# Score groups of two chunks in one visit of the dense layer, in a fused retention and gated layer kernel

## The chip, the cores and the metric

The kernel runs on one core of a Trainium2 chip. The metric is the device time of one launch in microseconds; a kernel's time is the median of several runs. One execution of each kernel was also taken by the hardware profiler, and the profile's span is the part of that execution from the first to the last instruction of the program.

## The reference

A retention layer (attention with a decay and without a softmax) over 8 batches of 8 heads, 576 positions and 64 features, then a dense layer with the activation h cos(h) over its 4608 tokens of 512 features:

```python
scores = scale * np.matmul(q, k.transpose(0, 1, 3, 2))
gamma = 1.0 - 2.0 ** (-5.0 - np.arange(H))
Dmat = np.where(rel >= 0, gamma[:, None, None] ** rel[None], 0.0)   # rel = i - j
attn = np.matmul(scores * Dmat[None], v)          # 8 x 8 x 576 x 64
x = attn.transpose(0, 2, 1, 3).reshape(4608, 512)
h = x @ w_in                                      # 512 -> 2048
out = (h * np.cos(h)) @ w_out                     # 2048 -> 512
```

## The kernel before

The positions of a batch are cut into five chunks, four of 128 and a last one of 64. The decay is split into a factor on v, a factor on the output and a causal mask, so that within a chunk the scores need only the mask, and everything before the chunk sits in a running state (k transposed times v, one 64 x 64 block a head).

For a chunk r of batch b there are two steps. `scores(b, r)` (line 405) is one group of eight TensorE matmuls, one a head, with 64 rows of contraction; the two heads of a pair sit on the two halves of the array and write two PSUM banks, sc0 and sc1. VectorE then multiplies each bank by the mask into a bf16 tile (line 428), `rt`, of which there are two pairs in turn. `rest(b, r)` (line 433) is the remainder: four matmuls of the state with q (tile names kqt, sb; not for chunk 0), eight of the masked scores with v (rt, vb), both into the bank po; eight that add the chunk to the state bank st (vb, kqb; not for chunk 4); two ScalarE copies of the state into SBUF (line 471) and one VectorE product that takes po into the token tile xt (line 476). `stage(b, r)` is `rest(b, r)` followed by `scores(b, r + 1)`.

The dense layer works in nine blocks of 512 tokens. `mlp1(j, dt)` (line 489), sixteen times a block, is four matmuls of w_in with xt into a bank, a ScalarE sine (line 504) and a VectorE product of the two into the tile gt (line 507). `mlp2(j, st, part)` (line 514) is four of the sixteen matmuls of one output tile of 128 tokens; four parts fill one bank, which ScalarE then copies out (line 538) for a store. Both take their banks from the four dense banks mm0 to mm3 in rotation:

```python
def bank(self):
    while self.n_mm % 4 in self.open.values():
        self.n_mm += 1
    self.n_mm += 1
    i = (self.n_mm - 1) % 4
    return self.MM[i], self.bMM[i]
```

`open` holds the bank of an output tile that is not complete; only such a bank is passed over. Before anything is written into a bank, its former readers must be done.

The order of each engine's instructions is the order in which the program emits them, and a helper adds the semaphore waits that the buffers call for. So the place of the retention work among the matmuls of the dense layer is written out by hand, in `emit`. In block j from 1 to 6 the batch b = j + 1 is worked on: the program runs mlp1 sixteen times, and then n = 0 to 15 output visits, `mlp2(j, n // 4, n % 4)`. Ahead of the visits n = 0, 3, 6, 9, 12 comes a part of batch b: at n = 0 the rest of the former batch's chunk 4 and the scores of chunk 0; at n = 3, 6, 9 and 12 the rest of chunk n/3 - 1 and the scores of chunk n/3. The document calls block j's part of the program stage j. Block 0 and the first two batches are ordered differently and are not touched.

Keys and queries of batches 2 to 7 reach their transposed form (tile kqt) by DMA: `prep` (line 320) casts a chunk on GpSimd and issues a transposing DMA on SyncE's queue (line 328). These run ahead of TensorE, in the order of batches and chunks, with every buffer doubled by the parity of the batch.

Of the kernel before, what the change touches and what calls it, by code (L numbers as in the profile page):

```python
# [16 lines left out]
NCH = (S_ + CH - 1) // CH  # L17
# [106 lines left out]
class _Kernel:  # L124
# [425 lines left out]
    def emit(self):  # L550
        s = self.s
        self.load("k", 0, 0)
        self.load_q0()
        for x, r in (("v", 0), ("k", 1), ("v", 1), ("k", 2), ("k", 3), ("v", 2), ("v", 3),
                     ("k", 4), ("v", 4)):
            self.load(x, 0, r)
        self.consts_a()
        for c in range(3):
            self.consts_b(c)
        for r in range(2):  # L560
            self.casts(0, r)
        self.cast("pool", "k", 0, 2)
        self.w_in_load(0)
        self.cast("pool", "k", 0, 3)
        self.w_in_load(1)
        for r in (2, 3):
            self.vmul("pool", 0, r)
            self.w_in_load(r)
        self.w_in_load(4)
        self.casts(0, 4)  # L570
        for i in range(NWO):
            w = self.w_out_load(i)
            if i == 0:
                for r in range(NCH):
                    for x in "kv":
                        self.load(x, 1, r, after=[w])
            if i == 1:
                self.load_qx(1)
        for r in range(NCH):
            self.casts(1, r)  # L580

        po, st = (self.PO, self.bPO), (self.ST, self.bST)
        self.spin(30, po)
        evict = self.turn_k_pe(0, 0, st, "dve")
        for c in range(NP):
            self.cast_q0(c)
        evict()
        for c in range(NP):
            self.turn_q(0, c, "act")
            self.spin((8, 5, 5, 16)[c], po)  # L590
        self.consts_b(3)
        self.scores(0, 0)
        self.spin(10, po)
        self.turn_k(0, 1)
        self.spin(8)
        self.rest(0, 0)
        self.scores(0, 1)
        self.spin(16)
        self.turn_k(0, 2)
        self.rest(0, 1)  # L600
        self.scores(0, 2)
        self.turn_k(0, 3)

        s.op("act", lambda e: e.activation(self.JUNK.ap(), self.C_PIH.ap(), AF.Sin), reads=[self.bC])  # L604
        self.spin(8)
        self.scores(0, 3, sc=[self.bank(), self.bank()])
        self.rest(0, 2)
        self.spin(4)
        self.rest(0, 3, self.bank())
        self.spin(8, po)  # L610

        for dt in range(16):
            self.mlp1(0, dt)
            if dt == 2:
                self.turn_k(0, 4)
            if dt == 4:
                self.scores(0, 4)
            if dt == 6:
                self.rest(0, 4)

        self.fetch(2)
        for r in range(NCH):
            self.feed(2, r, 3 if r == NCH - 1 else 1)
        spare = [(self.PO, self.bPO), (self.SC[0], self.bSC[0]), (self.SC[1], self.bSC[1]),
                 (self.ST, self.bST)]
        for n in range(16):
            self.mlp2(0, n % 4, n // 4)
            if n == 7:
                for c in range(NP):
                    self.turn_q(1, c, ("act", "dve")[c % 2], spare[c])  # L630
            if n in (8, 10):
                self.turn_k(1, n // 2 - 4, spare[0])
            if n in (9, 12):
                self.scores(1, n // 3 - 3)
            if n == 13:
                self.rest(1, 0)
            if n == 14:
                self.turn_k(1, 2, spare[0])
        self.flush()
        self.rest(1, 1)  # L640
        self.spin(10)

        n = 3 * 64 + CH
        for dt in range(16):
            self.mlp1(1, dt, 0, n)
            if dt in (1, 7, 13):
                self.scores(1, 2 + dt // 6, True)
            if dt in (3, 9):
                self.turn_k(1, 3 + dt // 6)
            if dt in (5, 11):  # L650
                self.rest(1, 2 + dt // 6)
        for dt in range(16):
            self.mlp1(1, dt, n, TB - n)
        for j in range(1, NTB):
            b = j + 1
            for dt in range(16 if j > 1 else 0):
                self.mlp1(j, dt)
                if b < B_ and dt % 3 == 2:
                    self.feed(b, dt // 3)
            for n in range(16):  # L660

                if n == 0 and b <= B_:
                    self.rest(b - 1, NCH - 1)
                if b < B_:
                    if n == 0:
                        self.scores(b, 0)
                    elif n % 3 == 0 and n < 15:
                        self.stage(b, n // 3 - 1)
                self.mlp2(j, n // 4, n % 4)
        self.flush()  # L670
        for name, (h, n) in s.dsem.items():
            if name[0] == "o":
                self.nc.scalar.wait_ge(h, n)
# [28 lines left out]
```

## Time and profile before

| | us |
|---|---|
| median of 3 runs (316.6 to 317.02) | 316.94 |
| the profiled execution | 316.4 |
| its span | 314.7 |
| TensorE matmuls busy | 303.5 |
| TensorE weight loads busy | 159.6 |
| VectorE busy | 174.1 |
| ScalarE busy | 162.3 |
| GpSimd busy | 93.1 |

How to read the lines that follow: PE is TensorE, PEld its weight loads, DVE VectorE, ACT ScalarE, POOL GpSimd and SP SyncE; L401 is line 401 of the kernel. `sc<-kqt` names the tile that is written and those that are read, with buffer numbers left out. All of TensorE's groups go through one helper, so lines 401 and 403 hold all matmuls but a group's last and the last, and the tiles tell them apart. Shapes such as 64*128 are the rows and columns of the array that the instruction uses. Matmuls are pipelined, so the shown durations of neighbours overlap; the distance between starts is the time that one takes from the next. A few matmul records are missing from the trace.

The stages in the span: the output visits of stage 1 begin at 73.9 us, of stage 2 at 106.5, of stage 3 at 139.1, of stage 4 at 171.7, of stage 5 at 204.4 and of stage 6 at 237.0. TensorE is busy 32.53 of the 33 us from 139 to 172.

### The profile page before, as it was taken

How to read it: one execution, taken by the hardware profiler on the slowest of the kernel's cores; microseconds unless marked ns; L12 is line 12 of the kernel's file. 1: busy time of each engine (PE TensorE's matmuls, PEld its weight loads, DVE VectorE, ACT ScalarE, POOL GpSimd, SP SyncE). 2: the span in 40 equal slices, each digit the busy share in tenths (PEclk: the TensorE clock that was granted, in tenths of full speed). 3: DMA queues.
4: the chain of work that ended last, by engine and by line, in shares of the span. 5: the costliest groups of instructions: out<-in, count | busy, mean ns of one | idle time of the engine just before them, and what ended most of it. 6: DMA issues, size and time to landing. Idle time of an engine off the chain costs nothing.

```text
span 314.7 us, 6424 instructions
## 1 busy us (share of the span) xinstructions
PE 303.5 (96%) x2516; PEld 159.6 (51%) x2552; DVE 174.1 (55%) x301; ACT 162.3 (52%) x290; POOL 93.1 (30%) x128
## 2 busy tenths in 40 slices
PE   6989999999999999999999999999999999999996
PEld 5754455666544455445544554455444544444442
DVE  3567624787527743685458644765387438405700
ACT  7566525785337533763277236723473257316711
POOL 2692027535454434453445424210000000000000
PEclk9999999999999999999999999999999999999999
DMA  7999999999999999999999999940001100120021
GB/s 218 213 168 204 203 220 247 264 192 209 212 256 183 217 210 247 217 224 217 259 208 202 225 204 221 172 85 35 33 0 38 66 33 0 42 94 1 12 83 74
DMA packets 142814, 48.85 MB, mean 155 GB/s; under 512 B 132544, under 2 KB 137664, under 8 KB 142784
## 3 DMA queue, kind: packets, MB, share of 16 engines
q1 hardware_dynamic: 132320, 34.22, 59.7%
q0 software_dynamic: 5280, 4.78, 9.5%
q10 hardware_dynamic: 5184, 9.44, 8.9%
q8 instruction: 20, 0.33, 0.4%
q14 instruction: 10, 0.08, 0.1%
HBM read 36.70 MB, written 9.44 MB: 147 GB/s over the span
## 4 chain that ended last, share of the span: by engine, by line
PE 90%; DMA 2%; DVE 2%; ACT 2%; issue 2%; SPq 1%; POOL 0%; DVEq 0%
PE mm L401 59%; PE mm L403 20%; PE po L401 6%; PE sc L401 4%; DMA kn<-in_k_dram 2%; PE st L401 1%; DVE gt L507 1%; DVE rt L428 1%; SPq L276 1%; ACT sb L471 0%; DVE xt L476 0%; ACT L604 0%; ACT osb L538 0%; ACT kqt L365 0%; SPq L267 0%
## 5 line engine op out<-in xcount | busy, mean ns | idle before, releaser
L507 DVE TENSOR_TENSOR gt<-mm,cb 128x512 bf16<-128x512 f32 (+2 forms) x160 | 101.1, 637 | 66.2 <-ACT cb L504 63.6
L401 PE MATMUL mm<-xt,win 128*128 128x512 bf16 (+2 forms) x468 | 116.0, 358 | 1.0 <-DVE xt L476 0.3
L504 ACT ACTIVATE cb<-mm,c_pih 128x512 bf16<-128x512 f32 (+2 forms) x160 | 101.9, 645 | 27.8 <-PE mm L403 27.0
L401 PE MATMUL mm<-wout,gt 128*128 128x512 bf16 x408 | 111.8, 380 | 2.3 <-issue 1.7
L401 PEld LDWEIGHTS mm<-xt,win 128*128 128x128 bf16 x480 | 44.6, 98 | 48.8 <-DVE gt L507 2.3
L401 PEld LDWEIGHTS mm<-wout,gt 128*128 128x128 bf16 x432 | 39.3, 98 | 45.1
L403 PE MATMUL mm<-xt,win 128*128 128x512 bf16 (+2 forms) x160 | 57.2, 358 | 0.3
L538 ACT ACTIVATE osb<-mm 128x512 f32<-128x512 f32 x36 | 21.5, 597 | 68.0 <-PE mm L403 68.0
L403 PE MATMUL mm<-wout,gt 128*128 128x512 bf16 x144 | 54.6, 379 | 0.5
L308 POOL TENSOR_TENSOR vb<-vn,wv 128x512 bf16<-128x512 f32 (+1 forms) x40 | 41.7, 1043 | 29.2 <-DMA vn<-in_v_dram 24.7
L428 DVE TENSOR_TENSOR rt<-sc,mk 128x512 bf16<-128x512 f32 (+1 forms) x78 | 45.8, 625 | 4.8 <-PE sc L403 4.8
L476 DVE TENSOR_TENSOR xt<-po,up 128x512 bf16<-128x512 f32 (+1 forms) x39 | 24.7, 634 | 41.9 <-PE po L403 41.8
L471 ACT ACTIVATE sb<-st 64x256 bf16<-64x256 f32 x64 | 24.2, 378 | 40.1 <-PE st L403 38.7
L318 POOL CAST kqb<-kn 128x512 bf16<-128x512 f32 (+1 forms) x40 | 24.4, 611 | 65.2 <-DMA kn<-in_k_dram 56.2
L318 POOL CAST kqb<-qn 128x512 bf16<-128x512 f32 (+1 forms) x30 | 18.5, 615 | 17.7 <-DMA qn<-in_q_dram 17.5
L403 PEld LDWEIGHTS mm<-xt,win 128*128 128x128 bf16 x160 | 15.7, 98 | 15.7
L403 PEld LDWEIGHTS mm<-wout,gt 128*128 128x128 bf16 x144 | 14.1, 98 | 17.0
L401 PE MATMUL po<-rt,vb 128*64 128x128 bf16 (+1 forms) x273 | 15.2, 220 | 0.0
L401 PE MATMUL sc<-kqt 64*128 64x128 bf16 (+1 forms) x273 | 14.7, 215 | 0.0
L401 PEld LDWEIGHTS po<-kqt,sb 128*128 128x128 bf16 x124 | 8.6, 98 | 7.8 <-DVE rt L428 1.6
L401 PEld LDWEIGHTS po<-rt,vb 128*64 128x64 bf16 (+1 forms) x273 | 9.3, 108 | 5.9 <-DVE rt L428 2.1
L401 PE MATMUL po<-kqt,sb 128*128 128x128 bf16 (+1 forms) x124 | 11.2, 213 | 0.4 <-DVE rt L428 0.2
(88 smaller groups left out, 133.2 us busy)
## 6 DMA issues: line engine op xcount, KB each, us to landing
out_dram<-osb ACTq DMA_DIRECT2D x36, 256.0 KB, 3.3
kn<-in_k_dram SPq DMA_DIRECT2D x32, 256.0 KB, 4.7
vn<-in_v_dram SPq DMA_DIRECT2D x32, 256.0 KB, 5.3
qn<-in_q_dram SPq DMA_DIRECT2D x24, 256.0 KB, 4.8
wout<-in_moe_w_out_dram POOLq DMA_DIRECT2D x4, 512.0 KB, 14.5
win<-in_moe_w_in_dram POOLq DMA_DIRECT2D x3, 512.0 KB, 8.2
qn<-in_q_dram SPq DMA_DIRECT2D x4, 288.0 KB, 4.7
kn<-in_k_dram SPq DMA_DIRECT2D x8, 128.0 KB, 3.5
```

The costliest lines, as they stand in the source:

```text
L276: s.dma("sp", f"q0_{c}", lambda e: e.dma_start(dst, src), writes=[self.bQN[c]])
L308: self.s.op(eng, lambda e: e.tensor_tensor(bass.AP(self.VB[i][r], 0, v3), self.staged("v", r, v3[1:]), bass.AP(self.WV, r * H_, [[NCH * H_ ...
L318: self.s.op(eng, lambda e: e.tensor_copy(o, f), reads=[self.bST32[x][r]], writes=[bt[i][r]])
L401: self.nc.tensor.matmul(o, a, b, **kw)
L403: return s.done("pe", self.nc.tensor.matmul(o, a, b, **kw), reads, writes)
L428: self.s.op("dve", lambda e: e.tensor_tensor(bass.AP(self.RT[k][hp], 0, p3), bass.AP(sc[0], 0, p3), bass.AP(self.MK, 0, [[CH, ck], [0, NP] ...
L471: s.op("act", lambda e: e.activation(bass.AP(self.SB[r % 2], 64 * hp * 512 + 64 * hp, [[512, 64], [128, NP], [1, D_]]), bass.AP(self.ST, 6 ...
L476: s.op("dve", lambda e: e.tensor_tensor(bass.AP(self.XT, t0, [[NP * XR, 128], [XR, NP], [1, ck]]), bass.AP(po, 0, [[512, 128], [CH, NP], [ ...
L504: s.op("act", lambda e: e.activation(co, mo, AF.Sin, bias=self.C_PIH.ap(), scale=1.0), reads=[bm, self.bC], writes=[bcb])
L507: s.op("dve", lambda e: e.tensor_tensor(bass.AP(g, dt * TB + o, [[16 * TB, 128], [1, n]]), mo, co, ALU.mult), reads=[bm, bcb], writes=[bg])
L538: s.op("act", lambda e: e.activation(o.ap(), m.ap(), AF.Copy), reads=[bm], writes=[bo])
```

## The change

From batch 2 on, the scores of two chunks are taken one behind the other: chunks 0 and 1 at n = 0, chunks 2 and 3 at n = 7, chunk 4 alone at n = 13. The second group of a pair takes its two banks from the four dense banks by `bank()`. The rests come at n = 4, 7, 10 and 13; the rest of chunk 4 stays at the next stage's n = 0.

```diff
                 if b < B_:
-                    if n == 0:
-                        self.scores(b, 0)
-                    elif n % 3 == 0 and n < 15:
-                        self.stage(b, n // 3 - 1)
+                    if n in (4, 7, 10, 13):
+                        self.rest(b, n // 3 - 1)
+                    if n in (0, 7):
+                        self.scores(b, n // 3)
+                        self.scores(b, n // 3 + 1, sc=[self.bank(), self.bank()])
+                    elif n == 13:
+                        self.scores(b, NCH - 1)
                 self.mlp2(j, n // 4, n % 4)
```

| n | before | changed |
|---|---|---|
| 0 | rest 4 of b - 1, scores 0 | rest 4 of b - 1, scores 0, scores 1 |
| 3 | rest 0, scores 1 | |
| 4 | | rest 0 |
| 6 | rest 1, scores 2 | |
| 7 | | rest 1, scores 2, scores 3 |
| 9 | rest 2, scores 3 | |
| 10 | | rest 2 |
| 12 | rest 3, scores 4 | |
| 13 | | rest 3, scores 4 |

In stages 1 to 6 the rotation then gives the second score group mm2 and mm3, output tiles 0 and 2 the bank mm0 and tiles 1 and 3 the bank mm1, where before the four output tiles had a bank each. No matmul, copy, product or DMA is added or dropped.

## The prediction

> **What bounds the kernel now.** I read the page first: busy shares, then the chain that ended last.
>
> ```profile
> span 314.7 us, 6424 instructions
> PE 303.5 (96%) x2516; PEld 159.6 (51%) x2552; DVE 174.1 (55%) x301; ACT 162.3 (52%) x290; POOL 93.1 (30%) x128
> ...
> PEclk9999999999999999999999999999999999999999
> ...
> PE 90%; DMA 2%; DVE 2%; ACT 2%; issue 2%; SPq 1%; POOL 0%; DVEq 0%
> PE mm L401 59%; PE mm L403 20%; PE po L401 6%; PE sc L401 4%; DMA kn<-in_k_dram 2%; PE st L401 1%; DVE gt L507 1%; DVE rt L428 1%; SPq L276 1%; ACT sb L471 0%; DVE xt L476 0%; ACT L604 0%; ACT osb L538 0%; ACT kqt L365 0%; SPq L267 0%
> ```
>
> TensorE makes 90% of the chain at the full granted clock; scores (sc) are 4% of it. Next, the waits of TensorE's two rows between 74 and 259 us, the stretch in which batches 2 to 7 run their chunk visits (stages 1 to 6):
>
> ```profile
> PE mm L401 <- issue: 1.6, 10, 0.2
> PE mm L401 <- DVE gt L507: 0.3, 2, 0.2
> ...
> PEld po L401 <- DVE rt L428: 2.1, 5, 0.4
> ```
>
> Twelve waits of the matmuls, none over 0.2 us: gaps of one missing matmul record each, with a little more, not stalls. The five before a weight load of po stand where n = 3 goes from the dense layer straight to rt matmuls; the masks had ended 0.25 us before. So there TensorE's time is the sum of its instructions and of what it loses between them, and a saving inside a visit reaches the end undiminished. That loss is in the timeline of TensorE, here the visits n = 0 and n = 3 of stage 4:
>
> ```profile
> 171.52 0.38 PE L403 MATMUL mm<-xt,win 128*128 128x512 bf16 x1
> 171.73 0.28 PE L401 MATMUL po<-kqt,sb 128*128 128x64 bf16 x4
> 171.94 0.31 PE L401 MATMUL po<-rt,vb 64*64 64x64 bf16 x7
> 172.06 0.19 PE L403 MATMUL po<-rt,vb 64*64 64x64 bf16 x1
> 172.19 0.39 PE L401 MATMUL sc<-kqt 64*128 64x128 bf16 x7
> 172.37 0.22 PE L403 MATMUL sc<-kqt 64*128 64x128 bf16 x1
> 172.52 0.82 PE L401 MATMUL mm<-wout,gt 128*128 128x512 bf16 x3
> ...
> 175.46 0.29 PE L401 MATMUL st<-vb,kqb 128*64 128x64 bf16 x7
> 175.55 0.20 PE L403 MATMUL st<-vb,kqb 128*64 128x64 bf16 x1
> 175.68 0.39 PE L401 MATMUL sc<-kqt 64*128 64x128 bf16 x7
> ```
>
> Columns: start, time, engine, line, names, array shape, count. Durations overlap, so I price by starts. A score group starts 172.19, its eighth matmul 172.37, the dense layer after it 172.52: a slot of 0.33. The eight run in pairs; the exact starts of the four pairs stand 0.066, 0.056 and 0.056 us apart. The step from the last pair to the dense layer is 0.148 instead of 0.056: leaving the 64*128 shape costs 0.09. From the last st to the scores it is 0.13 against 0.03 within st.
>
> **The change, part by part.** Per batch:
>
> 1. Visits n = 3 and n = 9 lose their score group (rest alone moves on to n = 4 and n = 10). Then st is followed by the dense layer instead of by scores. Does leaving st cost the same? The mixed layer of stage 1 has it:
>
> ```profile
> 59.97 0.20 PE L403 MATMUL st<-vb,kqb 128*64 128x64 bf16 x1
> 60.10 0.58 PE L401 MATMUL mm<-xt,win 128*128 128x320 bf16 x3
> ```
>
> 0.13 again. So each removes the whole slot: -0.330.
>
> 2. Visits n = 0 and n = 7 get a second group of eight behind the first in the same shape: four more pairs at 0.056 = +0.224. No row has two groups on end. From below, the eighth's start less the first's, 0.18, is all that a group could take if its first pair came free; from above 0.33, if the new group (other banks, a wait of its own) paid for leaving and entering like a separate one. I take 0.224: nothing changes shape between the groups, and po to st, two groups of one shape, step by 0.05 only.
>
> 3. n = 13 does what n = 12 did; the moved rests have the same dense neighbours. No matmul, copy, product or DMA is added or dropped.
>
> Sum: 2 x (0.224 - 0.330) = -0.21 per batch, six batches: **-1.27 us**. From the bounds: 12 x (0.18 - 0.33) = -1.8 and 12 x 0 = 0. The profiled execution took 316.4 (span 314.7 and 1.7 around it), so it would become 315.1; the median of the runs is 316.94, 0.54 above that execution, and becomes **315.67**.
>
> A page has a rule for the step: the Trainium skill, "TensorEngine Tiling (Array Packing)", section Key Properties, says that a change of tiling mode drains the engine, and "TensorE: Matmul & The Clock Gate", section Step-by-step, gives a drain about 128 cycles, which at 2.4 GHz is an estimate of 0.053 us. By that, twelve mode changes fewer bring 0.64 us; the row says 0.09 for one, and decides. Against the change speaks the second page's section "A second HAM failure mode": groups that cycle through PSUM banks, with small idle gaps between, let the clock be gated to half. The page's row of granted clock shows 9 in all 40 slices through sixty such visits, so I price it at nothing; one such window (3.4 us by the page) would cost 1.7 us and turn the sign.
>
> **New waits.** The second group uses two of the four dense banks. In stages 2 to 6 they are those of dt = 12 and 13, and the output matmuls of n = 0 now take the bank of dt = 14 instead of dt = 12; all of TensorE queues behind these. The gt product of dt = 14 ends at 172.55 in stage 4 (start 171.86, 0.69 long); TensorE's weight load follows a VectorE end by 0.05 in this trace (69.03 to 69.09). Needed then: 172.19 + 0.178 + 0.224 + 0.148 = 172.74. Slack 0.13, the same in stages 3, 5, 6; 0.36 in stage 1 (gt 74.47, need 74.88), and 0.03 in stage 2, where one gt product came 0.36 late (gt 107.41, need 107.50). So the cover is thin. If it is gone, each 0.1 us of lateness in all six costs 0.6. The second group itself waits for the gt of dt = 13, 0.7 us earlier, and has room.
>
> The second group also needs its transposed chunk earlier: chunk 1 at n = 0 instead of 3, chunk 3 at n = 7 instead of 9. Landing against new need: batch 2 chunk 1, 69.66 against 74.6; batch 2 chunk 3, 77.86 against 82.6; batch 3 chunk 1, 100.63 against 107.2; **batch 3 chunk 3, 113.80 against 115.15**, the closest; from batch 4 on over 11 us. Only that one, 7.7 us in flight where the median is 4.6, is near.
>
> Off the path: VectorE gets four masks in a row (2.4 us by 0.6 spacing) at n = 0, and rest of chunk 1 reads the last pair at n = 7, some 5 us later. ScalarE's state copies (0.78 a visit) are needed three visits (2.6 us) later, with one 0.60 eviction before them. At n = 8 and n = 12 the output matmuls take a bank for the second time; its eviction ended four visits earlier. SyncE's and GpSimd's queues keep their order; GpSimd's casts write buffers that the rests of two batches back still read, and two of these move by up to 0.86; the closest cast behind a moved rest starts 2.5 us after it (batch 7 chunk 0, 177.71 against 175.21), and batch 7's transposes land 35 us before use.
>
> **The rivals.**
>
> *The bank wait bites.* If the gt of dt = 14 reaches TensorE 0.1 to 0.2 us late in every stage, 0.6 to 1.2 come back: 316.3 to 316.9, say 316.6. For: slack of 0.03 to 0.13. Against: the VectorE starts are regular to 0.01 us in stages 3 to 6. Chance 0.10.
>
> *The second group pays full price* (its banks or its wait force TensorE through the same loss): 12 x 0, 316.9. For: no row shows it. Against: po to st. Chance 0.06.
>
> *A late transpose makes it slower.* The chunk 3 transpose of batch 3 is issued behind a full SyncE queue; before the change it had 4.1 us to spare, now 1.35. A landing 1.35 + 1.27 + 0.63 = 3.25 us later than here (11 us in flight) gives 317.6 or more. For: DMA is at 9 tenths there, and this landing was already the slowest of 30. Against: no landing took over 7.7. Each us beyond 115.15 costs a us; it decides from about 116.4. Chance 0.04.
>
> **How the numbers follow.** The forecast, 0.80: 315.67, its own range 315.2 to 316.1 (the three runs span 0.42; the lower bound of part 2 gives 315.1). The range reaches to the middle of the bank rival: **315.1 to 316.5**; the last two rivals stay mostly outside. 0.2% is 0.63 us, about what a measurement of this kernel can tell from no change, so faster means under 316.3: nearly all of the forecast (0.78) and the lower part of the bank rival (0.03). Within 0.2%: the rest of these, the full price rival and a transpose late by 1 to 2 us, 0.15. Slower, 0.04.
>
> **What would show it.** In the profile after: n = 0 has two score groups with 0.23 between their first starts and 0.15 from the last pair to the dense layer; n = 4 and n = 10 go from st to dense in 0.13; stages 2 to 6 are 0.21 us shorter each. A wait of the dense matmuls at n = 0 on VectorE's gt is the first rival, 0.33 between the groups the second, a wait for kqt at n = 7 of stage 2 the third. A stage shortened by less than 0.1, or a new gap in the dense layer that follows, would prove me wrong.

## The result, and the profile after

| | before | changed |
|---|---|---|
| median of 11 runs on one chip, us | 317.02 (316.6 to 317.44) | 315.71 (315.09 to 316.52) |
| the profiled execution, us | 316.4 | 315.09 |
| its span, us | 314.7 | 313.3 |

The ratio is 0.996 with a 95% interval of 0.9949 to 0.9971: the changed kernel is 0.3 to 0.5% faster, 1.31 us by the medians.

The chain of the changed kernel's page has the same order of lines, with the score groups' share down from 4% to 2%:

```profile
PE mm L401 60%; PE mm L403 20%; PE po L401 6%; DMA vn<-in_v_dram 3%; PE sc L401 2%; PE st L401 1%; ACT cb L504 1%; DVE rt L428 1%; SPq L276 1%; DVE gt L507 0%; SPq L267 0%; DVE xt L476 0%; ACT osb L538 0%; ACT kqt L365 0%; POOL vb L308 0%
```

Most of that fall is only a name: the twelve second groups now write dense banks and count under mm. The stretches say where the time went. Cut at the first matmul of n = 0 and at the first of the next block's mlp1, the output visits of stages 3 and 4 stood before at

```profile
139.11:157.92 18.81, 18.44 (x190) 10.04 (x192) 9.91 (x17) 5.54 (x13) 8.42 (x11) 1.00 1.12 236
171.73:190.54 18.81, 18.44 (x190) 10.04 (x192) 9.92 (x17) 5.54 (x13) 6.73 (x10) 1.00 1.10 218
sum 112.86, PE 110.64 PEld 60.24 DVE 59.29 ACT 33.06 POOL 33.49; mean PE 18.44 PEld 10.04 DVE 9.88 ACT 5.51 POOL 5.58
```

and after at

```profile
138.62:157.22 18.60, 18.12 (x191) 10.03 (x192) 9.92 (x17) 5.42 (x13) 8.45 (x11) 1.00 1.17 231
171.03:189.62 18.59, 18.11 (x190) 10.03 (x192) 9.92 (x17) 5.42 (x13) 7.67 (x11) 1.00 1.18 230
sum 111.57, PE 108.71 PEld 60.20 DVE 59.30 ACT 32.34 POOL 34.22; mean PE 18.12 PEld 10.03 DVE 9.88 ACT 5.39 POOL 5.70
```

Columns: stretch, length, busy time of TensorE, its weight loads, VectorE, ScalarE and GpSimd with their instructions, granted clock, DMA share, GB/s. The sums are over stages 1 to 6. All six are 0.21 to 0.22 us shorter, 112.86 - 111.57 = 1.29 us together, with the same weight loads and the same clock. The dense stretches between them (13.81) and the tail did not change. So the span's 1.34 us less are these 1.29 and 0.06 ahead of stage 1, where the two kernels are alike.

The timeline of TensorE at n = 0 and n = 4 of stage 4:

```profile
171.49 0.39 PE L401 MATMUL sc<-kqt 64*128 64x128 bf16 x7
171.67 0.22 PE L403 MATMUL sc<-kqt 64*128 64x128 bf16 x1
171.72 0.38 PE L401 MATMUL mm<-kqt 64*128 64x128 bf16 x7
171.89 0.22 PE L403 MATMUL mm<-kqt 64*128 64x128 bf16 x1
172.27 0.59 PE L401 MATMUL mm<-wout,gt 128*128 128x512 bf16 x2 [0.16 <-issue]
...
175.84 0.29 PE L401 MATMUL st<-vb,kqb 128*64 128x64 bf16 x7
175.94 0.20 PE L403 MATMUL st<-vb,kqb 128*64 128x64 bf16 x1
176.07 0.60 PE L401 MATMUL mm<-wout,gt 128*128 128x512 bf16 x2
```

The second group (mm<-kqt) starts 0.05 after the last pair of the first, where the dense layer used to start after 0.15. At n = 4 st goes to the dense layer in 0.13. (The first dense matmul's record at n = 0 is missing, hence x2 and the gap; the x2 of the last row is where the window ends.) The waits of TensorE from 73 to 259 us:

```profile
PE mm L401 <- issue: 2.7, 17, 0.2
PE mm L401 <- DVE gt L507: 0.2, 1, 0.2
...
PEld po L401 <- DVE rt L428: 2.1, 5, 0.4
```

There is no new wait: the eighteen gaps of the matmuls are again of the size of one missing record. The run with the first pair alone, further down, has the same pair at n = 0 and all its records; there TensorE's matmuls show no gap at all in this stretch, and the dense layer starts 0.15 after the pair.

### The profile page after: what moved, and what is told of

The parts are those of the page before. It is cut to its first block, busy times and chain, and to the rows that moved or that the text cites. A ratio compares the mean times of both kernels' runs of the same rounds, so it can differ in the third digit from the quotient of the medians.

```text
span 313.3 us, 6427 instructions
## 1 busy us (share of the span) xinstructions
PE 301.7 (96%) x2519; PEld 159.8 (51%) x2552; DVE 174.2 (56%) x301; ACT 161.7 (52%) x290; POOL 93.2 (30%) x128
## 4 chain that ended last, share of the span: by engine, by line
PE 90%; DMA 3%; issue 2%; ACT 2%; DVE 2%; SPq 1%; POOL 1%; DVEq 0%
PE mm L401 60%; PE mm L403 20%; PE po L401 6%; DMA vn<-in_v_dram 3%; PE sc L401 2%; PE st L401 1%; ACT cb L504 1%; DVE rt L428 1%; SPq L276 1%; DVE gt L507 0%; SPq L267 0%; DVE xt L476 0%; ACT osb L538 0%; ACT kqt L365 0%; POOL vb L308 0%
## 5 line engine op out<-in xcount | busy, mean ns | idle before, releaser
L428 DVE TENSOR_TENSOR rt<-sc,mk 128x512 bf16<-128x512 f32 (+1 forms) x54 | 30.5, 600 | 4.8 <-PE sc L403 4.8
L428 DVE TENSOR_TENSOR rt<-mm,mk 128x512 bf16<-128x512 f32 x26 | 16.6, 682 | 0.1
```

What stands on the lines that cost most here:

```text
L428: self.s.op("dve", lambda e: e.tensor_tensor(bass.AP(self.RT[k][hp], 0, p3), bass.AP(sc[0], 0, p3), bass.AP(self.MK, 0, [[CH, ck], [0, NP] ...
```

## The experiments

All edits are made to the changed kernel's loop. Times are medians with before on the same chip and in the same set of runs beside them; "stage" is the length of a stage's output visits in the profile, which repeats to 0.01 us from stage to stage and so tells apart what the totals can't: the total moves with what happens ahead of stage 1, which begins between 73.7 and 75.4 us in these profiles.

**The rests moved, nothing paired.**

```diff
-                    if n in (0, 7):
+                    if n in (0, 4, 7, 10, 13):
                         self.scores(b, n // 3)
-                        self.scores(b, n // 3 + 1, sc=[self.bank(), self.bank()])
-                    elif n == 13:
-                        self.scores(b, NCH - 1)
```

> The rests move to n = 4, 7, 10 and 13 as in the change, but each chunk's scores are taken alone behind the rest, in sc0 and sc1. Theory of the array's shape (what is saved is leaving the 64*128 shape twelve times less, 0.106 us each): no saving, the time of before, 316.8 to 317.2, output visits of a stage 18.81 us long. Rival, the place (the saving comes from later rests and their waits): 315.7, stages 18.6 us long.

317.23 against 317.01, ratio 1.0002 (0.9987 to 1.0018). Its stage 3:

```profile
139.33:158.14 18.81, 18.81 (x193) 10.05 (x192) 9.91 (x17) 5.42 (x13) 8.43 (x11) 1.00 1.21 211
```

18.81, as before; the place of the rests brings nothing. All matmul records are there in this stage, and TensorE is shown busy for its whole length: there was no gap to be saved.

**The pair split by one visit.**

```diff
                     if n in (0, 7):
                         self.scores(b, n // 3)
+                    elif n in (1, 8):
                         self.scores(b, n // 3 + 1, sc=[self.bank(), self.bank()])
```

> As the change, but the second group of a pair comes one output visit later (n = 1 and n = 8), so that four dense matmuls stand between the two. Theory of the shape: a group between dense matmuls costs 0.094 to enter and 0.330, so 0.424 where the change pays 0.224 and before 0.330: 12 x 0.094 = 1.13 us slower than before, 318.1. Rival, the dense banks or the earlier scores bring the gain: 315.7 as the change.

317.92 against 317.01, ratio 1.0035 (1.0021 to 1.0049), stages 19.02. With the second group again in two dense banks (at n = 1 one further on in the rotation) and chunk 1's scores nearly as early, the gain is gone and turns into a loss of 0.21 a stage. The timeline at n = 1 of stage 4:

```profile
173.67 0.38 PE L403 MATMUL mm<-wout,gt 128*128 128x512 bf16 x1
173.99 0.39 PE L401 MATMUL mm<-kqt 64*128 64x128 bf16 x7
174.17 0.22 PE L403 MATMUL mm<-kqt 64*128 64x128 bf16 x1
174.31 0.61 PE L401 MATMUL mm<-wout,gt 128*128 128x512 bf16 x2
```

By the exact starts it is 0.31 into the group, instead of the dense layer's own 0.22, and 0.15 out of it. It is the neighbourhood of the groups that counts.

**One matmul of another shape, or of the same, between the groups of a pair.**

```diff
+                        sc = [self.bank(), self.bank()]
+                        m, bm = sc[0]
+                        idt = bass.AP(self.ID, 0, [[128, K], [1, 128]])   # K = 128, or 64
+                        self.group([(bass.AP(m, 0, [[512, 128], [1, 128]]), idt, idt,
+                                     dict(start=True, stop=True))], [self.bID], [bm])
-                        self.scores(b, n // 3 + 1, sc=[self.bank(), self.bank()])
+                        self.scores(b, n // 3 + 1, sc=sc)
```

K = 128:

> As the change, with one 128*128 identity matmul of 128 columns between the two groups of each pair (twelve in all; it writes the bank that the second group then overwrites). Theory of the shape: 0.148 to leave, 0.056 for it, 0.094 to enter again, in place of one step of 0.056: 0.24 each, 2.9 us more than the change, 318.6. Rival, the loss belongs to the group and its wait and not to the shape: 0.056 each, 0.7 us more, 316.4.

K = 64:

> As the kernel with the 128*128 matmul between the groups of a pair, but the matmul between has the groups' own shape, 64*128, with the identity's upper 64 rows. Theory of the shape: one step of 0.056 at most, 12 times: 0.7 us more than the change, 316.4. Rival, any foreign matmul between the groups brings the loss back: 0.24 each as the 128*128 one is to cost, 318.6.

With 128 rows: 319.09 against 317.01, ratio 1.0063 (1.0046 to 1.0081), stages 19.13, which is 0.27 more for each of the twelve matmuls (0.24 was expected). With 64 rows: 316.01 against 316.76, ratio 0.9981 (0.9963 to 0.9999), stages 18.70, 0.05 more for each. The same place, the same banks, the same waits; only the shape differs. The timelines at n = 0 of stage 4, first with 128 rows:

```profile
173.36 0.22 PE L403 MATMUL sc<-kqt 64*128 64x128 bf16 x1
173.51 0.23 PE L403 MATMUL mm<-ident 128*128 128x128 bf16 x1
173.68 0.40 PE L401 MATMUL mm<-kqt 64*128 64x128 bf16 x7
```

then with 64:

```profile
172.33 0.22 PE L403 MATMUL sc<-kqt 64*128 64x128 bf16 x1
172.38 0.22 PE L403 MATMUL mm<-ident 64*128 64x128 bf16 x1
172.38 0.38 PE L401 MATMUL mm<-kqt 64*128 64x128 bf16 x6
```

By the exact starts it is 0.15 and 0.16 around the foreign matmul; 0.05 and nothing around the like one, beside which the next group's first matmul on the other half of the array even runs. This ties the loss to the change of shape.

**The first pair alone.**

```diff
-                    if n in (0, 7):
+                    if n in (0, 7, 10):
                         self.scores(b, n // 3)
-                        self.scores(b, n // 3 + 1, sc=[self.bank(), self.bank()])
+                    if n == 0:
+                        self.scores(b, 1, sc=[self.bank(), self.bank()])
```

> As the change, but only chunks 0 and 1 are paired; chunks 2, 3 and 4 follow their rests at n = 7, 10 and 13 alone. Theory of the shape: six pairs of twelve, 0.106 each: 0.64 us faster than before, 316.4, output visits of a stage 18.70 us long. Rival, one of the two visits carries the gain: 315.7 or 317.0.

316.24 against 316.76, ratio 0.9985 (0.9971 to 0.9998), stages 18.70: half of the gain, 0.11 a pair.

**One bank passed over at n = 0.**

```diff
+                    if n == 0:
+                        self.bank()
                 self.mlp2(j, n // 4, n % 4)
```

> As the change, but one dense bank is passed over at n = 0, so that the output matmuls of n = 0 take the bank of dt = 15 instead of dt = 14. If the bank's last reader decides: gt of dt = 15 ends 0.86 us after that of dt = 14, the slack was 0.13, so each of stages 2 to 6 stalls 0.73 us less than nothing else hides, and stage 1 about 0.1: 3.8 us more than the change, 319.5. Rival, the wait is hidden by what TensorE has queued: 315.7.

319.31 against 317.01, ratio 1.0076 (1.0061 to 1.009). Stage 1 takes 18.73, stages 2 to 6 19.33: 0.13 and 0.73 more than the change, 3.8 in all. The waits of TensorE's matmuls in that trace, and the place in stage 4:

```profile
PE mm L401 <- DVE gt L507: 3.3, 5, 0.7
```

```profile
174.04 0.22 PE L403 MATMUL mm<-kqt 64*128 64x128 bf16 x1
174.92 0.61 PE L401 MATMUL mm<-wout,gt 128*128 128x512 bf16 x2 [0.66 <-DVE gt L507]
```

The gt of dt = 15 starts at 174.17 and takes 0.69, so TensorE goes on 0.06 after its end. The wait is not cushioned by anything: what the next dense bank costs is the difference of two ends, and the change is just on the free side of it.

**Pairs across batches.** The gain should grow if chunk 4 is paired too. In stages 3 and 5 chunk 4 is taken with the next batch's chunk 0, in stages 4 and 6 then chunks 1 and 2, and 3 and 4:

```diff
+                ahead = b in (4, 6)
-                if b < B_:
+                if b < B_ and b not in (5, 7):
...
                     elif n == 13:
                         self.scores(b, NCH - 1)
+                        if ahead:
+                            self.scores(b + 1, 0, sc=[self.bank(), self.bank()])
+                elif b < B_:
+                    if n in (3, 6, 9, 12):
+                        self.rest(b, n // 3 - 1)
+                    if n in (3, 9):
+                        self.scores(b, n // 3)
+                        self.scores(b, n // 3 + 1, sc=[self.bank(), self.bank()])
                 self.mlp2(j, n // 4, n % 4)
+                if n == 15 and ahead:
+                    self.n_mm += 2
```

> A version that could beat both: as the change, and in stages 3 and 5 chunk 4 at n = 13 is paired with the next batch's chunk 0, whose transposed keys landed 7 us or more earlier in the trace of before; stages 4 and 6 then pair chunks 1 and 2 at n = 3 and chunks 3 and 4 at n = 9, with rests at n = 3, 6, 9 and 12. Two groups less stand alone: 2 x 0.106 = 0.21 us less than the change, 315.5. Rival, the extra masks on VectorE at n = 13 or the banks delay the next dense layer: 315.7 or more.

The last two lines of the edit keep the rotation of the banks in step. In this kernel the scores of chunk 0 of batches 5 and 7 are taken from the keys and queries of two batches earlier, since the program brings the new ones only afterwards; the amount of work is the same. 315.86 against 316.76, ratio 0.9985 (0.9966 to 1.0004). Stages 3 and 4 take 18.92 and 18.37, 37.29 together where the change takes 37.19. No gain, and the timeline at n = 13 of stage 3 shows why, with the groups of chunk 4 and chunk 0:

```profile
154.37 0.31 PE L401 MATMUL sc<-kqt 64*64 64x64 bf16 x7
154.49 0.19 PE L403 MATMUL sc<-kqt 64*64 64x64 bf16 x1
154.61 0.40 PE L401 MATMUL mm<-kqt 64*128 64x128 bf16 x7
```

Chunk 4 has 64 keys, so its matmuls use 64*64 of the array, and the step of 0.12 to the next group is that of a change of shape, not the 0.03 of one pair of 64 columns.

With the new keys brought first (the feed of the next batch's chunk 0 is moved ahead of its scores):

```diff
-                if b < B_ and dt % 3 == 2:
+                if b < B_ and dt % 3 == 2 and (b not in (5, 7) or dt > 2):
                     self.feed(b, dt // 3)
...
                         if ahead:
+                            self.feed(b + 1, 0)
```

> The version with pairs across batches once more, with the next batch's chunk 0 fetched, cast and transposed by the program before its scores are taken. In the trace of the former run the step from chunk 4's scores (64*64) to chunk 0's (64*128) took 0.125 like a change of shape. Theory of the shape, with 64*64 a shape of its own: over stages 3 and 4 there are seven runs of score groups of one shape against six in the change, so 0.106 more a two stages, 37.29 us of output visits against 37.19, and about 315.9 in all. Rival, it is the order of keys and masks that cost there: with the transposes in place the two stages take 36.98, and 315.5.

315.62 against 317.13, ratio 0.9945 (0.9925 to 0.9964), stages 3 and 4 again 18.92 and 18.37. The stages are those of the theory; the total is no worse than the change's, but the two were not run side by side and 0.2 us is less than such intervals resolve.

Then chunk 4 in the larger shape:

```diff
+        wide = b > 1 and r == NCH - 1
+        kc = CH if wide else ck
...
-                    bass.AP(sc[hp][0], c * CH, [[512, ck], [1, ck]]),
-                    bass.AP(self.KQT[i], base, [[TP, 64], [1, ck]]),
+                    bass.AP(sc[hp][0], c * CH, [[512, kc], [1, ck]]),
+                    bass.AP(self.KQT[i], base, [[TP, 64], [1, kc]]),
...
+        more = [self.bKT[i][0], self.bQT[i][0]] if wide else []
-        self.group(mms, [self.bKT[i][r], self.bQT[i][r]], [sc[0][1], sc[1][1]])
+        self.group(mms, [self.bKT[i][r], self.bQT[i][r]] + more, [sc[0][1], sc[1][1]])
```

> As the kernel with pairs across batches, but from batch 2 on chunk 4's scores load 128 columns of keys instead of 64 (the further 64 are the next head pair's chunk 0 or queries, and the 64 rows that they give are not read), so that they run in the 64*128 shape. Theory of the shape: chunk 4 then shares a run with its neighbour; five runs over stages 3 and 4 against six in the change, 37.08 us of output visits against 37.19, and 315.5 in all, 0.2 less than the change. Rival, the smaller output or the other batch's operands cost the step and not the shape: 37.29.

315.13 against 317.13, ratio 0.9935 (0.9913 to 0.9957). The profile of this run spans 1086.3 us and gives no stages; they are read from a second run of the same kernel, with the change on the same chip:

> The kernel with pairs across batches and chunk 4's scores in the 64*128 shape again, since its profiled execution was disturbed as a whole. Theory of the shape: output visits of stages 3 and 4 together 37.08 us, 0.11 less than the change, and 0.2 less in all. Rival: 37.29, as with the 64*64 shape.

> The changed kernel once more, beside the kernel with pairs across batches and the wide chunk 4 on one chip: 37.19 us for the output visits of stages 3 and 4, and 0.2 us more than that kernel by the theory of the shape, 0.2 less by the rival.

This kernel 315.37, ratio 0.9945 (0.9922 to 0.9968); the change 315.60, ratio 0.9956 (0.9933 to 0.9979); before 316.84. The change's stages 3 and 4 are 37.19 again. Those of this kernel:

```profile
138.90:157.70 18.80, 18.32 (x198) 10.17 (x200) 11.11 (x19) 5.41 (x13) 8.28 (x11) 1.00 1.20 238
171.52:189.76 18.24, 17.92 (x183) 9.77 (x184) 8.71 (x15) 5.52 (x13) 7.16 (x11) 1.00 1.09 235
sum 37.04, PE 36.25 PEld 19.94 DVE 19.82 ACT 10.93 POOL 15.44; mean PE 18.12 PEld 9.97 DVE 9.91 ACT 5.47 POOL 7.72
```

37.04, 0.15 less than the change and 0.25 less than with the 64*64 shape, at the step

```profile
154.66 0.29 PE L401 MATMUL sc<-kqt 64*128 64x64 bf16 x7
154.76 0.19 PE L403 MATMUL sc<-kqt 64*128 64x64 bf16 x1
154.78 0.38 PE L401 MATMUL mm<-kqt 64*128 64x128 bf16 x7
```

0.03 where it was 0.12, although the columns that stream, the banks and the other batch's operands are the same. Of the 0.15, the pair brings the expected 0.11. The rest is chunk 4's own: in stages 1 and 2, where it stands alone in the larger shape, the output visits take 0.02 less a stage than in the change. Over the six stages it comes to 0.3 us less than the change; the totals (315.37 and 315.60) lean that way but don't separate the two. Against before, the interval (0.9922 to 0.9968) leaves it faster.

## Why the prediction was right

The forecast was 1.27 us less; the medians say 1.31, with 0.9 to 1.6 by the interval, and the profiles' six stages 1.29. That the median of 315.71 lies 0.04 from the forecast 315.67 is luck, for the eleven runs of the change spread over 1.4 us; the stages, 0.21 shorter each as forecast, are what the mechanism is tested by.

1. *A lone group's slot of 0.330 goes.* Held: st to the dense layer takes 0.13 at n = 4, as it did to the scores at n = 3.
2. *A second group costs 0.224.* Held: from the first group's start to the second's is 0.234, the later pairs step by 0.05 to 0.06, and per pair the stage is 0.107 shorter (0.215 / 2) against the forecast 0.106. The upper bound, 0.33 for a group with banks and a wait of its own, is what the same group costs when a matmul of another shape stands ahead of it, so the bound had the right size but the wrong condition: it is the change of shape that brings it, not the banks or the wait.
3. *The moved rests cost nothing.* Held: 18.81 with the rests moved alone.

The rivals. *The bank wait* did not bite: in stage 4 of the changed kernel the gt of dt = 14 ends at 171.85 and the dense matmul starts at 172.05 (the recorded one at 172.27 less a step of 0.22). In stage 2, where the forecast left 0.03, that gt ends at 107.14 and the weight load of the dense matmul starts at 107.22, 0.08 later, where one that does wait follows by 0.05; the stage is as short as the others, but only just. The slack was read rightly from the trace of before, for the bank one further on cost 0.73 a stage, as its end foretold. *The full price for the second group* is refuted by the change's own timeline (0.23 between the groups, not 0.33) and by the pair of experiments with a matmul between. *The late transpose* did not come: batch 3's chunk 3 landed at 112.86 and was used at 114.88 in the profiled execution. In all eight profiles of kernels with that pair at n = 7 it landed 1.2 to 3.5 us ahead of its use; other executions left no trace.

The estimate of 0.053 us for a change of mode, which the prediction works out from the Trainium skill ("TensorE: Matmul & The Clock Gate", section "Step-by-step: what each phase is for"), would have made 0.64 us of it; the measured 0.107 is twice that. Nor did the clock fall: the granted clock is 1.00 in all six stages. The section "A second HAM failure mode" of the same page, cited against the change, would have had it gated at times; this trace does not show that. (The prediction's "sixty such visits" are thirty in stages 1 to 6, five a stage.)

That the cause is the change of array shape, and not the place, the banks or the waits, was argued in the prediction; the experiments show it. Groups set apart, or with another shape between them, lose the gain; with the same shape between them they lose only that matmul's own step; and chunk 4 joins in once it has its neighbour's shape. One change is worth 0.09 to 0.10 on top of the ordinary step. Most of the rest of the 0.107 is the first pair of a group, which steps by 0.066 instead of 0.056 behind a change.

## What to carry to other kernels

Where TensorE is the bound, price a group of small matmuls by the distance from its first start to the start of what follows, not by its duration, and put groups that use the same rows and columns of the array next to each other; each change of shape that is spared was worth 0.1 us here. Before pairing, look at the shape column: a ragged last tile may have a shape of its own, and loading full columns for it can be cheaper than the change. And when a regrouping takes banks from a rotation, compare the end of the new bank's last reader with the new need, for that wait comes through unhidden.

## What was not expected of the hardware

64*64 and 64*128 count as different shapes: the step between their groups was 0.12 us, and 0.03 once both used 64*128, with the smaller matmul streaming the same 64 columns. The change from st's 128*64 to 64*128 cost no more than that from 64*128 to the dense layer's 128*128 (0.13 and 0.15 from the last start, 0.03 and 0.06 of it the ordinary step): whether one dimension changes or both made little difference.

Where the time goes at a change can be seen in the rows of the weight loads, here at n = 0 of stage 3 of the kernel before:

```profile
138.90 0.38 PE L403 MATMUL mm<-xt,win 128*128 128x512 bf16 x1
138.90 0.37 PEld L401 LDWEIGHTS po<-kqt,sb 128*128 128x128 bf16 x4
139.11 0.28 PE L401 MATMUL po<-kqt,sb 128*128 128x64 bf16 x4
...
139.44 0.19 PE L403 MATMUL po<-rt,vb 64*64 64x64 bf16 x1
139.56 0.22 PEld L401 LDWEIGHTS sc<-kqt 64*128 64x128 bf16 x7
139.57 0.39 PE L401 MATMUL sc<-kqt 64*128 64x128 bf16 x7
```

Within one shape (mm to po) the next weight load starts together with the matmul before it, 0.21 ahead of its own matmul. At a change of shape (64*64 to 64*128) it starts only 0.12 after the last matmul of the old shape, 0.01 ahead of its own. The 0.09 to 0.10 that a change costs is also about what one weight load takes in these rows, 0.09 to 0.11. Whether the load that no longer runs ahead is the whole cost, or the array pauses for a reason of its own and the load with it, no run here separates.
